# Rows of maxima from ScalarE's queue, seven projection steps a round, and gaps that end with a query group

## The chip, the cores and the metric

One core of one Trainium2 chip runs the kernel. The metric is the device time of one execution in microseconds; the runs shown are a median of three. Engines are called as in the profile: PE is TensorE (PEld its weight loads), DVE is VectorE, ACT is ScalarE, POOL is GpSimd, SP is SyncE, which issues most DMAs. A name with a q behind it (SPq, ACTq) is the engine's instruction queue.

## The reference

Four residual layers on one sequence of 2048 tokens with 576 features: sliding-window attention, a spectral filter, and both again with the same weights.

```python
def _A_ref(x, wqkv, wo):
    H = 32; Dh = D // H; W = 256                     # D = 576, Dh = 18
    qkv = (x @ wqkv).reshape(B, S, 3, H, Dh)          # -> q, k, v
    scores = einsum("bhqd,bhkd->bhqk", q, k) * (Dh ** -0.5)
    mask = (0 <= idx_q - idx_k) & (idx_q - idx_k < W)
    p = softmax(where(mask, scores, -1e9))
    return einsum("bhqk,bhkd->bhqd", p, v).reshape(B, S, D) @ wo

def _B_ref(x, w_r, w_i):
    X = rfft2(x) * (w_r + 1j * w_i)
    return irfft2(X, s=(S, D))

x = x + _A_ref(_layernorm(x), wqkv, wo)
x = x + _B_ref(_layernorm(x), w_r, w_i)
x = x + _A_ref(_layernorm(x), wqkv, wo)
x = x + _B_ref(_layernorm(x), w_r, w_i)
```

## The kernel before, in words

The attention layer (`layer_a`) is called twice; the spectral layer (`layer_b`) follows each. Only `layer_a` is touched.

**Tiles and head groups.** The 32 heads are worked in 8 groups `n` of four heads; a head of a group is named by `pair` and `hp`. The sequence has 16 tiles of 128 tokens. A tile of a group has a running number `x` = 16·n + i, 128 in all. Four tiles make a chunk `c` of 512 tokens.

**Projections.** A list `pj` holds the matmuls that make q and k: one *group* of 14 steps (128×512 each, line 798) for each block of 128 columns (i) and chunk (c). The groups of i = 0 and 1 are done first; the other 28 groups, 392 steps, are in `pj`. After its last step ScalarE casts the group to a high part `sg` (line 810), and a closure is put aside that subtracts on VectorE (line 813) and writes both parts to DRAM as `qk_d` (line 815, from ScalarE's queue for i < 2, otherwise from SP's). `remainders` calls the closures put aside. `stack_load` (line 830) brings q and k of one head group and chunk back from DRAM to `qs` and `ks`: twelve DMAs from SP.

**Scores, twice.** `score_max` (S, line 855) multiplies q by k for 128 queries and up to 384 keys, and VectorE takes each query's maximum (line 857). When four tiles of a chunk have their maxima, `m_rows` (line 865) transposes them on TensorE (`tpm`), ScalarE negates them into `mt` (line 870), and four DMAs of 2 KB (line 875) put them as one more row into `qs`, for each of the four heads. `exps` (E, line 892) then multiplies k by q with that row, which subtracts the maximum, and ScalarE takes the exponential (line 893); GpSimd cuts the two edges of the window (lines 895, 898). The maxima run ahead of the exponentials by `LEAD` = 10 tiles.

**Values.** `part` (line 912) adds one tile's products of P and V into the PSUM bank U. Four tiles of queries make a query group; at its end ScalarE copies U to `us` (line 917), and the next group writes U again. `norm` (line 926) transposes `us`, divides and stores.

**Order of the work.** The order is written out by hand. Every engine works its instructions in program order.
- `opening` (line 966): ten rounds, each with the four S of one tile and a share of the projection steps; before, 75 steps in ten rounds, eight and seven in turn. `m_rows` for chunks 0 and 1 of group 0 comes at the ends of rounds 4 and 8 (counted from 0).
- `bursts` (line 992): 158 bursts `k`, each of one S, three E, two S, and then a filling: value parts in some bursts, otherwise projection steps (14 to a gap of two to four bursts; in the first gap, bursts 0 to 3, nine steps), with at most two tasks (`m_rows` or `norm`) after the first two steps. `m_rows` for chunk 2 of group 0 is the task of burst 3, that for chunk 3 of burst 8. Bursts 4, 7, 9, ... hold value parts. When the projections are used up, from burst 137 on, parts are spread over all bursts, up to a length of 430 a burst (`took`).
- After them the last tiles (x ≥ 118), then the output projection (`Out`), which runs on into the spectral layer.

**Banks.** PSUM tags: `E` and `S` have three banks each, `pj` and `U` one. `turned` (line 860) chooses the bank of the transposes by how many steps are `done`: `E` before 75, then `S`, and `pj` when the projections are over. Group (i = 3, c = 0), the fifth of `pj`, stands in an `E` bank until its remainder has been taken.

Of the kernel before, what the change touches and what calls it, by code (L numbers as in the profile page):

```python
# [8 lines left out]
F32 = mybir.dt.float32  # L9
# [6 lines left out]
S, D = 2048, 576  # L16
DF = 289
NF = 290
NT = 16
# [589 lines left out]
def layer_a(tc, ident, eps, bp, src, dst, wqk_d, wv_d, wo_d, dc_d, gc_d, dram, copy, wvs, second, spectral, share):  # L609

    nc = tc.nc
# [15 lines left out]
    if True:  # L627
# [134 lines left out]
        with ExitStack() as c2:  # L762
# [9 lines left out]
            for j in range(2):  # L772
                q = wp.tile([128, 2, S], F32R, name=f"qs{j}", bufs=1)
                k = wp.tile([128, 2, S], F32R, name=f"ks{j}", bufs=1)
# [5 lines left out]
            def remainders():  # L780
                while ended:
                    ended.pop(0)()
# [60 lines left out]
            def score_max(x, pair, hp):  # L843

                n, i = divmod(x, NT)
                c, t = divmod(i, 4)
                q, k = qs[n % 2], ks_[n % 2]
                if (n, c) not in ms:
                    ms[n, c] = wp.tile([128, 2, 2, 4], F32, tag="m", name=f"m{n}_{c}", bufs=3)
                lo, hi = max(0, i - 2) * 128, (i + 1) * 128  # L850
                N = hi - lo
                b = 64 * hp
                four = x < LEAD and pair == hp == 1
                ps = pp.tile([128, 512], F32, tag="U" if four else "S", name=f"S{x}_{pair}_{hp}", bufs=1 if four else 3)
                T.matmul(ps[:, 0:N], q[b:b + 63, pair, i * 128:i * 128 + 128], k[b:b + 63, pair, lo:hi], start=True, stop=True)  # L855
                jk = wp.tile([128, 384], BF, tag="jk", name=f"jk{x}_{pair}_{hp}", bufs=3)
                V.tensor_tensor_reduce(out=jk[:, 0:N], in0=ps[:, 0:N], in1=mask[:, 384 - N:384], scale=1.0, scalar=-3e38,  # L857
                                       op0=ALU.add, op1=ALU.max, accum_out=ms[n, c][:, hp, pair, t:t + 1])

            def turned(name):  # L860

                tag = "E" if done < 75 else "S" if done < len(pj) else "pj"
                return pp.tile([128, 4, 128], F32, tag=tag, name=name, bufs=1 if tag == "pj" else 3)

            def m_rows(n, c):
                q = qs[n % 2]
                tp = turned(f"tpm{n}_{c}")
                T.transpose(tp[0:16, 0], ms[n, c].rearrange("p a b t -> p (a b t)"), ident)
                mt = wp.tile([16, 128], F32R, tag="mt", name=f"mt{n}_{c}", bufs=2)
                A.activation(mt, tp[0:16, 0], AF.Copy, scale=-1.0)  # L870
                for hp in range(2):
                    for pair in range(2):
                        r = (hp * 2 + pair) * 4
                        b = 64 * hp + 63
                        nc.sync.dma_start(q[b:b + 1, pair, c * 512:c * 512 + 512].rearrange("a (t q) -> a t q", t=4).bitcast(F32),
                                          mt[r:r + 4].bitcast(F32))

            pt = {}
# [70 lines left out]
            LEAD = 10  # L949
            pj = [f for i in range(2, 9) for c in range(4) for f in proj(i, c, c % 2 if i == 2 else c == 0 and i == 3)]  # L950
            done, due = 0, []
# [3 lines left out]
            def loads(t):  # L955
                if t + LEAD in (0, 2):
                    stack_load(0, 2 + (t + LEAD) // 2)
                n, c = divmod(t + 20, NT)
                if c % 4 == 0 and 0 < n < NQ:
                    stack_load(n, c // 4)  # L960
                if t + LEAD == 5:
                    v_load(0)
                if t + 12 in range(NT, NX, NT):
                    v_load((t + 12) // NT)

            def opening():

                n = 0
                for t in range(-LEAD, 0):
                    loads(t)  # L970
                    for pair in range(2):
                        for hp in range(2):
                            score_max(t + LEAD, pair, hp)
                    remainders()
                    want = -(-75 * (t + LEAD + 1) // LEAD)
                    yield from pj[n:want]
                    n = want
                    y = t + LEAD - 1
                    if y > 0 and y % 4 == 3:
                        m_rows(0, y // 4)  # L980

            def lasting(p):
                x, half = p
                i = x % NT
                return 0 if i == 0 else 216 if half else 432

            def source(p):
                x, half = p
                i = x % NT
                return x - 1 if half == 0 else x - 2 + 2 * (i % 2)  # L990

            def bursts():

                es = [(x, pair, hp) for x in range(MIX) for pair in range(2) for hp in range(2)]
                ss = [(x + LEAD, pair, 1 - hp) for x, pair, hp in es]
                parts = [(x, half) for x in range(MIX - 2) for half in range(2) if x % NT]
                values = {(4 * x + 7) // 3 + 2 for x in range(0, MIX - 2, 2)}
                ends = [3] + [max(k - 1 for k in values if k - 1 <= 4 + 134 * (i + 1) // 22) for i in range(22)]
                steps = {}
                for i, end in enumerate(ends):  # L1000
                    ks = [k for k in range(ends[i - 1] + 1 if i else 0, end + 1) if k not in values]
                    m = 14 if i else 9
                    steps.update({k: m // len(ks) + (z < m % len(ks)) for z, k in enumerate(ks)})
                at = 75
                for k in range(-(-len(es) // 3)):
                    e, c = es[3 * k:3 * k + 3], ss[3 * k:3 * k + 3]
                    for x, pair, hp in e:
                        if pair == hp == 0:
                            loads(x)
                            assert not any(source(p) == x - 6 for p in parts)  # L1010
                    score_max(*c[0])
                    for f in e:
                        exps(*f)
                    for f in c[:0:-1]:
                        score_max(*f)
                    remainders()

                    new, took = [], 0
                    spread = at == len(pj)
                    while parts and (took < 430 or source(parts[0]) < e[0][0] - 3 if spread else took == 0 or parts[0][0] % 2 or parts[0][1]):  # L1020
                        if (4 * source(parts[0] if spread else (parts[0][0] | 1, 1)) + 3) // 3 + 2 > k:
                            break
                        x, half = parts.pop(0)
                        part(x, half)
                        took += lasting((x, half))
                        if half and x % 4 == 3:
                            new.append((norm, *divmod(x // 4, 4)))

                    due.sort(key=lambda z: z[0] is norm)
                    tasks = [] if took and not spread else due[:1 + (len(due) > 2)]  # L1030
                    del due[:len(tasks)]
                    n = steps.get(k, 0)
                    for f in pj[at:at + min(2, n)]:
                        yield f
                    for f, *a in tasks:
                        f(*a)
                    for f in pj[at + 2:at + n]:
                        yield f
                    at += n

                    full = (3 * k + len(e)) // 4 + LEAD - 1
                    if (3 * k) // 4 + LEAD - 1 < full and full % 4 == 3:
                        new.append((m_rows, *divmod(full // 4, 4)))
                    due.extend(new)
                    for x, pair, hp in e:
                        if pair == hp == 1:
                            behind(x)
                remainders()
                assert at == len(pj)
                for p in parts:  # L1050
                    part(*p)
                    if p[1] and p[0] % 4 == 3:
                        due.append((norm, *divmod(p[0] // 4, 4)))
# [32 lines left out]
            for f in opening():  # L1086
                f()
                done += 1
            U = pp.tile([128, 512], F32, tag="U", name="U", bufs=1)
            V.memset(U, 0.0)  # L1090
            for f in bursts():
                f()
                done += 1
# [89 lines left out]
```

## Time and profile before

| | |
|---|---|
| median of 3 runs | 1512.99 us (1512.7 to 1518.36) |
| the profiled execution | 1514.61 us |
| its span, first to last instruction | 1512.9 us |
| mean granted clock of TensorE | 0.988 |
| busy: PE, PEld, DVE, ACT, POOL | 95%, 73%, 64%, 52%, 41% |
| first attention layer: opening and bursts | from about 107 to 458 us |
| second attention layer: opening and bursts | from about 858 to 1210 us |

A timeline row has the start in us, the length in us, engine, line, operation, the tile written and the tile read, their shapes, how many instructions were merged, and in brackets the idle time before it with what ended it. A row by stretches has, for each engine, the busy time in us and the number of instructions in brackets, then the granted clock (1.00 is full), the mean busy share of the 16 DMA engines and GB/s. A row of one line's instructions has the shortest, the median and the longest duration in ns. In the page's groups of instructions the count is followed by the busy time in us, the mean length in ns, and the idle time before them with what ended most of it.

### The profile page before, as it was taken

Reading aid. Unit: us, or ns where it says so; the run is one execution under the profiler, and the core shown is the slowest. Engines: PE = TensorE matmul, PEld = TensorE weight load, DVE = VectorE, ACT = ScalarE, POOL = GpSimd, SP = SyncE. Lnnn points to the kernel's source line nnn. Section 1 sums busy time; section 2 is a strip of 40 time slices with the busy share of each in tenths; the row PEclk is TensorE's granted clock in tenths of the full one; section 3 lists DMA queues with packets and bytes.
Section 4 is the critical chain, followed back from the end, with each engine's and each line's share of the span. In section 5 each row is a group of like instructions: output and inputs, shape, how many; then the busy total and the mean of one; then the engine's idle time right before and its main releaser. Section 6 shows DMA issues by size and latency. Waiting matters only on the chain.

```text
span 1512.9 us, 34671 instructions
## 1 busy us (share of the span) xinstructions
PE 1441.3 (95%) x12124; PEld 1097.8 (73%) x12124; DVE 968.4 (64%) x3152; ACT 789.3 (52%) x1900; POOL 623.0 (41%) x1026
## 2 busy tenths in 40 slices
PE   7998999999999899999999989999999998999998
PEld 7975666666656799759999756666666467997698
DVE  5327787878883555457852468878788735555476
ACT  5522676666676444224454246667666654442243
POOL 2172445445455323153421824444443543322434
PEclk9998999999999999999999989999999999999999
DMA  6756556655545365767663565555544454657654
GB/s 193 200 167 207 166 160 197 186 170 168 159 143 164 111 215 187 233 213 239 244 173 92 186 209 159 166 158 157 156 146 136 122 160 139 209 188 246 211 200 142
DMA packets 203131, 267.64 MB, mean 177 GB/s; under 512 B 103182, under 2 KB 108302, under 8 KB 201998
## 3 DMA queue, kind: packets, MB, share of 16 engines
q1 hardware_dynamic: 194638, 245.44, 52.6%
q10 hardware_dynamic: 7680, 15.59, 3.0%
q0 software_dynamic: 640, 4.39, 1.1%
q8 instruction: 97, 1.59, 0.5%
q14 instruction: 76, 0.62, 0.1%
HBM read 166.71 MB, written 102.00 MB: 178 GB/s over the span
## 4 chain that ended last, share of the span: by engine, by line
PE 70%; DVE 7%; DMA 6%; ACT 4%; POOL 4%; issue 2%; SPq 1%; POOLq 0%; DVEq 0%; ACTq 0%
PE pj L798 15%; PE S L855 12%; PE U L912 11%; PE ops L555 6%; PE E L892 5%; PE vps L738 4%; PE pf L202 3%; PE pz L215 3%; PE pi L361 2%; PE tpo L926 2%; PE po L382 2%; DMA ofree<-yd 1%; DMA qs<-mt 1%; PE pq L313 1%; PE p L294 1%
## 5 line engine op out<-in xcount | busy, mean ns | idle before, releaser
L857 DVE CUSTOM_DVE_ANT_0 jk<-S,mask 128x384 bf16<-128x384 f32 (+2 forms) x1024 | 491.2, 529 | 134.7 <-PE E L892 74.7
L893 ACT ACTIVATE P<-E 128x384 f32<-128x384 f32 (+2 forms) x1024 | 409.1, 475 | 180.5 <-PE E L892 151.9
L895 POOL TENSOR_SCALAR_AFFINE_SELECT P<-P 128x512 f32<-128x512 f32 x256 | 162.4, 634 | 386.9 <-ACT P L893 353.4
L855 PE MATMUL S<-ks,qs 63*128 63x384 f32 (+2 forms) x1024 | 281.4, 375 | 1.7 <-DVE m L857 0.5
L892 PE MATMUL E<-qs,ks 64*128 64x384 f32 (+2 forms) x1024 | 222.4, 374 | 12.1 <-DMA qs<-mt 10.0
L855 PEld LDWEIGHTS S<-ks,qs 63*128 63x128 f32 x1024 | 144.5, 187 | 114.2 <-DVE m L857 74.3
L912 PE MATMUL U<-P,vq 128*19 128x128 f32 (+1 forms) x3840 | 190.4, 331 | 4.4 <-ACT us L917 2.7
L798 PE MATMUL pj<-xh,wqh 128*128 128x512 f32 x360 | 156.8, 435 | 2.5 <-ACT vt L742 1.7
L912 PEld LDWEIGHTS U<-P,vq 128*19 128x19 f32 x3840 | 96.1, 99 | 82.4 <-issue 22.6
L898 POOL TENSOR_SCALAR_AFFINE_SELECT P<-P 128x512 f32<-128x512 f32 x224 | 142.0, 634 | 0.0
L892 PEld LDWEIGHTS E<-qs,ks 64*128 64x128 f32 x1024 | 110.9, 187 | 25.5 <-issue 13.8
L798 PE MATMUL pj<-xh,wql 128*128 128x512 f32 x360 | 128.1, 425 | 0.7 <-POOL wql L460 0.7
L555 PE MATMUL ops<-oroom 128*128 128x288 f32 x840 | 120.8, 299 | 4.4 <-DVE oroom L538 3.0
L798 PE MATMUL pj<-xl,wqh 128*128 128x512 f32 x288 | 120.1, 417 | 0.0
L555 PEld LDWEIGHTS ops<-oroom 128*128 128x128 f32 x840 | 112.8, 189 | 6.2 <-DVE oroom L538 3.9
L798 PEld LDWEIGHTS pj<-xh,wqh 128*128 128x128 f32 x360 | 67.9, 189 | 34.3 <-issue 11.4
L171 POOL TENSOR_TENSOR eo<-xn 128x287 f32<-128x287 f32 x32 | 26.1, 817 | 152.9 <-ACT xn L169 141.8
L813 DVE TENSOR_TENSOR sg<-pj,sg 128x512 fp32r<-128x512 f32 x72 | 49.5, 687 | 58.3 <-ACT sg L810 58.3
L857 DVE DVE_READ_ACCUMULATOR2_ANT m<- 128x1 f32 x1024 | 84.8, 83 | 0.0
L361 PE MATMUL pi<-oroom 128*128 128x256 f32 (+1 forms) x576 | 77.4, 289 | 5.9 <-ACT oroom L346 4.7
L798 PEld LDWEIGHTS pj<-xh,wql 128*128 128x128 f32 x360 | 64.2, 190 | 24.2 <-issue 12.8
L361 PEld LDWEIGHTS pi<-oroom 128*128 128x128 f32 (+1 forms) x576 | 73.1, 187 | 7.6 <-ACT oroom L346 5.6
(177 smaller groups left out, 2569.0 us busy)
## 6 DMA issues: line engine op xcount, KB each, us to landing
qk_d<-sg SPq DMA_DIRECT2D x56, 512.0 KB
qs<-qk_d SPq DMA_DIRECT2D x384, 72.0 KB
ks<-qk_d SPq DMA_DIRECT2D x384, 72.0 KB
v_d<-vt SPq DMA_DIRECT2D x32, 304.0 KB
vq<-v_d SPq DMA_DIRECT2D x16, 608.0 KB
yd<-ye SPq DMA_DIRECT2D x32, 290.0 KB
wt<-in_w SPq DMA_DIRECT2D x16, 580.0 KB
x<-ofree SPq DMA_DIRECT2D x32, 288.0 KB
```

The lines of the kernel that those rows point to most:

```text
L361: T.matmul(o, z[:, sl, c, lo:lo + m], mo, start=k == 0, stop=k == 5)
L555: self.nc.tensor.matmul(self.ps[u][n][:, 0:288], x, self.w[p][:, wk * D + n * 288:wk * D + n * 288 + 288], start=first and i == 0, stop=la ...
L738: T.matmul(ps[:, n, 0:288], xT(xk, c), w[:, wk, n * 288:(n + 1) * 288], start=i == 0, stop=i == len(ks) - 1)
L798: T.matmul(box["ps"].rearrange("r (n p) -> r n p", n=NT) if second else box["ps"], w[:, wk], x, start=s == 0, stop=s == len(ks) - 1)
L813: V.tensor_sub(rest[:, 1], by, rest[:, 0].bitcast(F32))
L855: T.matmul(ps[:, 0:N], q[b:b + 63, pair, i * 128:i * 128 + 128], k[b:b + 63, pair, lo:hi], start=True, stop=True)
L857: V.tensor_tensor_reduce(out=jk[:, 0:N], in0=ps[:, 0:N], in1=mask[:, 384 - N:384], scale=1.0, scalar=-3e38, op0=ALU.add, op1=ALU.max, accu ...
L892: T.matmul(ps[:, 0:nq], k[b:b + 64, pair, j * 128:j * 128 + 128], q[b:b + 64, pair, j * 128:j * 128 + nq], start=True, stop=True)
L893: A.activation(p[:, hl_, 0:nq], ps[:, 0:nq], AF.Exp, scale=SC)
L895: P.affine_select(out=p[:, :, 0:128], in_=p[:, :, 0:128], pattern=[[0, 4], [1, 128]], compare_op=ALU.is_ge, fill=0.0, base=0, channel_mult ...
L898: P.affine_select(out=p[:, :, 256:384], in_=p[:, :, 256:384], pattern=[[0, 4], [-1, 128]], compare_op=ALU.is_gt, fill=0.0, base=0, channel ...
L912: T.matmul(U[32 * h:32 * h + 19, (q0 % 4) * 128:(q0 % 4) * 128 + 128 * (q1 - q0)], vts[n][:, j, h], pt[n, j][:, h, (q0 - j) * 128:(q1 - j) ...
```

## The change

Three edits in `layer_a`.
- `m_rows`: the four DMAs of a row are issued by ScalarE when the head group is 0 and the chunk is 0, 1 or 2; by SP otherwise.
- `opening` and `bursts`: seven projection steps in each of the ten rounds (70 in all), and 14 in the first gap (four, four, three and three in bursts 0 to 3) as in the others. `turned` and the start of the bursts' counter go from 75 to 70 with it.
- `bursts`: a gap with value parts already in it ends before the first half of a tile that opens a query group (x % 4 == 0) or a head group's first computed tile (x % 16 == 1).

```diff
-                tag = "E" if done < 75 else "S" if done < len(pj) else "pj"
+                tag = "E" if done < 70 else "S" if done < len(pj) else "pj"
...
-                        nc.sync.dma_start(q[b:b + 1, pair, c * 512:c * 512 + 512].rearrange("a (t q) -> a t q", t=4).bitcast(F32),
+                        (nc.sync if n or c == 3 else nc.scalar).dma_start(q[b:b + 1, pair, c * 512:c * 512 + 512].rearrange("a (t q) -> a t q", t=4).bitcast(F32),
                                           mt[r:r + 4].bitcast(F32))
...
-                    want = -(-75 * (t + LEAD + 1) // LEAD)
+                    want = 7 * (t + LEAD + 1)
...
-                    m = 14 if i else 9
-                    steps.update({k: m // len(ks) + (z < m % len(ks)) for z, k in enumerate(ks)})
-                at = 75
+                    steps.update({k: 14 // len(ks) + (z < 14 % len(ks)) for z, k in enumerate(ks)})
+                at = 70
...
-                        x, half = parts.pop(0)
+                        x, half = parts[0]
+                        if took and half == 0 and (x % 4 == 0 or x % NT == 1):
+                            break
+                        parts.pop(0)
                         part(x, half)
```

## The prediction

> **What bounds the kernel now.** I read the page first: the chain of work that ended last, by engine, and the groups of instructions with what ended the idle time before them.
>
> ```profile
> PE 70%; DVE 7%; DMA 6%; ACT 4%; POOL 4%; issue 2%; SPq 1%; POOLq 0%; DVEq 0%; ACTq 0%
> L892 PE MATMUL E<-qs,ks 64*128 64x384 f32 (+2 forms) x1024 | 222.4, 374 | 12.1 <-DMA qs<-mt 10.0
> ```
>
> TensorE carries 70% of the chain, and the change neither adds nor removes a matmul. So only two things can move the time: holes in TensorE's row, and the clock at which it works. The second line names one hole that the change touches: 10.0 us in which E (the scores that go to the exponential) waited for the rows of maxima, which travel as `qs<-mt`. The timeline of TensorE shows where it lies, once in each attention layer:
>
> ```profile
> 137.59 0.62 PE L892 MATMUL E<-qs,ks 64*128 64x384 f32 x2
> 142.68 0.66 PE L892 MATMUL E<-qs,ks 64*128 64x384 f32 x1 [4.47 <-DMA qs<-mt]
> ...
> 891.78 0.65 PE L892 MATMUL E<-qs,ks 64*128 64x384 f32 x1 [5.07 <-DMA qs<-mt]
> ```
>
> That E is the ninth of its layer (burst 2, third of the burst): the first one that reads query tile 4, so the first that needs row group c=1. The timelines of ScalarE and of SyncE's queue show why the row is late:
>
> ```profile
> 130.87 0.27 ACT L870 ACTIVATE mt<-tpm 16x128 fp32r<-16x128 f32 x1 [3.01 <-PE tpm L868]
> ...
> 130.77 2.17 SPq L830 DMA_DIRECT2D qs<-qk_d  x6
> 132.99 3.23 SPq L830 DMA_DIRECT2D ks<-qk_d  x6
> 136.42 0.90 SPq L815 DMA_DIRECT2D qk_d<-sg  x2
> 137.41 3.30 SPq L875 DMA_DIRECT2D qs<-mt  x4
> ...
> 879.24 0.27 ACT L870 ACTIVATE mt<-tpm 16x128 fp32r<-16x128 f32 x1 [3.10 <-PE tpm L868]
> 887.47 3.29 SPq L875 DMA_DIRECT2D qs<-mt  x4
> ```
>
> The row is ready in SBUF at 131.14 (130.87 + 0.27). Its four DMAs stand in SP's queue behind twelve loads of the next head group and two writes of projections, and are issued from 137.41 to 140.71. TensorE goes on at 142.68, 1.97 us after the last issue. In the second layer 7.96 us pass between 879.51 and 887.47. So the wait is made on the queue, not by the transfer.
>
> The stretches by granted clock show a second loss behind the first:
>
> ```profile
> 141.00:142.00 1.00, 0.00 (x0) 0.00 (x0) 0.00 (x0) 0.00 (x0) 0.00 (x0) 0.60 0.26 94
> 150.00:151.00 1.00, 1.00 (x10) 0.82 (x6) 0.57 (x2) 0.16 (x1) 0.00 (x0) 0.50 0.01 3
> ...
> 888.00:889.00 1.00, 0.00 (x0) 0.00 (x0) 0.00 (x0) 0.00 (x0) 0.77 (x2) 0.85 1.04 358
> 898.00:899.00 1.00, 1.00 (x16) 0.35 (x8) 1.00 (x5) 0.51 (x2) 0.00 (x0) 0.53 0.52 199
> ```
>
> The columns are TensorE, weight loads, VectorE, ScalarE, GpSimd, then the clock, the DMA share and GB/s. During the wait the clock falls to 0.50, and it stays there to past 151 and near 899, long after work has resumed: 8.3 us of work at half speed in the first layer (142.68 to 151) and 7.2 us in the second.
>
> **The change part by part.** (1) *Queue.* For head group 0 the rows c=0, 1, 2 leave from ScalarE. With c=1 no longer behind SP's loads, the issue can begin at about 131.1. SP in turn gets to its loads about 3 us earlier each time it passes such a row; nothing on an engine waits for those loads in this stretch. c=0 was in time before and can only come earlier; c=3 stays on SP, where it was in time. The price of one issue:
>
> ```profile
> L815 SPq DMA_DIRECT2D qk_d<-sg x56: 365/389/2587, 125.4 to 1178.5; - x56
> L815 ACTq DMA_DIRECT2D qk_d<-sg x16: 361/366/404, 88.4 to 857.8; - x16
> L875 SPq DMA_DIRECT2D qs<-mt x256: 572/573/2399, 127.3 to 1217.2; - x128
> ```
>
> No row shows `qs<-mt` on ScalarE. The like transfer costs the same on both engines (389 against 366 ns), so I take SP's median, 573 ns, plus about 45 ns between two: four take 2.5 us. The ends are 1.5 us (four of 366 ns) and 9.6 us (four of SP's longest, 2399 ns). With 2.5 us of issue and the 1.97 us to landing, c=1 lands near 135.6, before burst 2 wants it at about 138. The two stalls go: −4.47 and −5.07 us.
>
> The Trainium skill, "DMA: Bandwidth & Descriptors", section "Issuing engines are not separate DMA queues", speaks against this: all issuers share the same 16 DMA engines, and a second issuer saves only sequencer time, usually small. Here sequencer time is the larger part, 6.27 us from 131.14 to 137.41 against 1.97 us to landing; by the page's "usually" the gain would be little, and no row of before shows this DMA on the other queue.
>
> (2) *Clock.* If the hole goes, so does the slow stretch. Burst starts (the single S at the head of each) price it:
>
> ```profile
> 144.74 0.69 PE L855 MATMUL S<-ks,qs 63*128 63x384 f32 x1
> 147.36 0.69 PE L855 MATMUL S<-ks,qs 63*128 63x384 f32 x1
> ...
> 150.08 0.69 PE L855 MATMUL S<-ks,qs 63*128 63x384 f32 x1
> 152.74 0.44 PE L855 MATMUL S<-ks,qs 63*128 63x384 f32 x1
> 154.82 0.44 PE L855 MATMUL S<-ks,qs 63*128 63x384 f32 x1
> ```
>
> Bursts 5 and 6 both hold five projection steps: 2.66 us, most of it slow, against 2.08 at full clock. Burst 3 took 2.62 us and burst 4 2.72; at full clock I estimate 1.7 (two steps and the row's transpose: 2.08 less three steps of 0.26, rounded up for the transpose and for what VectorE needs) and 1.85 (16 U, some 1.1 us by the rows of U in (5), in place of five steps). The rest of burst 2 (142.68 to 144.74) took 2.06, about 1.1 at full clock. Together 0.58 + 0.92 + 0.87 + 0.96 = 3.3; I take −3.0 in the first layer, and −2.7 in the second, where burst 5 is fast already. The ends are 0 and half of the slow work, −4.2 and −3.6.
>
> The Trainium skill, "TensorE: Matmul & The Clock Gate", section "What's actually happening", has the clock return after one busy window of about 3.4 us. By it the slow work would be worth at most half of 3.4 us, 1.7 a layer. The trace disagrees: 8.3 us.
>
> (3) *The new load on ScalarE.* Its queue is in order, so what stands behind an issue waits. c=0 and c=1 fall into the opening, where ScalarE idles (3.01 us ahead of the row above). Behind c=1 stand one cast of a projection and the first exponential; the issues end about 0.4 us after the cast could start. c=2 falls into burst 3:
>
> ```profile
> 147.25 0.58 ACT L810 CAST sg<-pj 128x512 fp32r<-128x512 f32 x1 [0.50 <-PE pj L798]
> 147.74 0.26 ACT L870 ACTIVATE mt<-tpm 16x128 fp32r<-16x128 f32 x1
> ...
> 150.84 1.26 ACT L893 ACTIVATE P<-E 128x384 f32<-128x384 f32 x3 [1.46 <-PE E L892]
> 153.25 1.26 ACT L893 ACTIVATE P<-E 128x384 f32<-128x384 f32 x3 [1.16 <-PE E L892]
> ```
>
> Burst 3 now has three steps with the row's transpose after the second, so the cast too comes behind the four issues: the three exponentials of burst 4 start 2.5 + 0.6 = 3.1 us later than the row's own end. E has three banks, so burst 5's first E waits for burst 4's first exponential. ScalarE's slack is 1.16 to 1.46 us a burst. I take 3.1 less about 1.1: +2.0 us a layer. The ends: 0 if the queue takes the issues beside other work, and +8.5 (9.6 less 1.1).
>
> (4) *Seven steps a round.* The opening loses five steps. Three heads of its rounds, the first wait of burst 0, and the page's groups of VectorE:
>
> ```profile
> 123.10 0.62 PE L855 MATMUL S<-ks,qs 63*128 63x384 f32 x4
> 125.72 0.62 PE L855 MATMUL S<-ks,qs 63*128 63x384 f32 x4
> 128.08 0.62 PE L855 MATMUL S<-ks,qs 63*128 63x384 f32 x4
> 134.17 0.44 PE L892 MATMUL E<-qs,ks 64*128 64x384 f32 x1 [0.43 <-ACT P L893]
> ...
> L857 DVE CUSTOM_DVE_ANT_0 jk<-S,mask 128x384 bf16<-128x384 f32 (+2 forms) x1024 | 491.2, 529 | 134.7 <-PE E L892 74.7
> L813 DVE TENSOR_TENSOR sg<-pj,sg 128x512 fp32r<-128x512 f32 x72 | 49.5, 687 | 58.3 <-ACT sg L810 58.3
> ```
>
> Eight steps make 2.62 us, seven 2.36: 0.26 a step, −1.3 in all. VectorE needs four maxima of 0.48 us (491.2 over 1024) and, every second round, 0.69 for a remainder: 2.27 on average, so it stays just under 2.36. The same five steps come back in bursts 0 to 3, +1.3 less what holes there swallow: 0.43 us in burst 0, where E waits for an exponential to free its bank, and perhaps as much in burst 1. ScalarE's 0.4 us from (3) eats part of it. I count (4) as 0; ends −0.9 (two such holes filled) and +0.4. From burst 4 on the steps lie where they lay.
>
> (5) *Gaps that end with a query group.* By the loop's own conditions the order changes only in bursts 141 to 150 of each layer, after the projections. There two bursts of a layer start the next group's part right behind the last part of the one before, and wait for U to be copied (both of the first layer, and the first of the second):
>
> ```profile
> 431.71 0.63 PE L912 MATMUL U<-P,vq 128*19 128x256 f32 x8 [0.85 <-ACT us L917]
> 440.05 0.63 PE L912 MATMUL U<-P,vq 128*19 128x256 f32 x8 [0.85 <-POOL P L898]
> ...
> 1182.20 1.05 PE L912 MATMUL U<-P,vq 128*19 128x256 f32 x8 [0.85 <-ACT us L917]
> ```
>
> At most −1.7 us a layer. Against it: two parts move into burst 150, which had none, and there ScalarE is full:
>
> ```profile
> 451.00:452.00 1.00, 1.00 (x11) 0.39 (x11) 0.86 (x5) 1.00 (x4) 1.00 (x2) 1.00 0.00 0
> ```
>
> I take −1.0 a layer; ends −1.7 and +0.6 (one part of 0.63 that nothing hides).
>
> **Sum.** First layer: −4.47 − 3.0 + 2.0 + 0 − 1.0 = −6.5. Second: −5.07 − 2.7 + 2.0 + 0 − 1.0 = −6.8. Together −13.3 us. The profiled execution took 1514.61 us with a span of 1512.9; I expect a span near 1499.6. The median of the runs shown, 1512.99, is 1.6 below the profiled execution; taken from it, the forecast is **1499.7**.
>
> **Rivals.**
> - *Issues cost ScalarE nothing that TensorE sees.* Then the +2.0 goes in both layers: 1495.7. For it: idle time of over 1 us a burst. Against: the cast stands behind the issues too. 14%.
> - *The new wait slows the clock.* A hole of 2 us in burst 5 could be enough, as holes of that sum were in the second layer:
>
> ```profile
> 1179.00:1182.00 3.00, 1.84 (x14) 0.91 (x14) 2.16 (x10) 2.29 (x6) 1.22 (x2) 1.00 0.79 228
> 1183.00:1185.00 2.00, 2.00 (x22) 1.31 (x22) 1.02 (x3) 1.06 (x3) 0.06 (x1) 0.50 0.44 156
> ```
>
> TensorE was busy 1.84 of 3 us and then ran at 0.50. About 1.5 to 2 us a layer: 1503.2. 17%. By the skill's clock page, same section, a whole idle window is needed and this rival would not occur; these two rows speak against that.
> - *The change does not do what it says:* the rows land late on the other queue as well, because the DMA engines are full of the loads that SP now issues earlier (share 1.04 at 888). If the stall is still 2 us with its slow clock, 9.5 − 4 and half of the clock term remain, and −5.5 − 2.9 + 4.0 − 2.0 = −6.4: 1506.6. 9%.
> - *Slower:* each of the four issues takes SP's longest, 2.4 us, on ScalarE. Then c=1 holds it 9.6 us and the first exponential is 7 us late, c=2 another 8.5, with slow clock behind both (3 each). A layer gains 8.6 ((1), (2) and (5)) and loses 7 + 8.5 + 6 = 21.5: +26 in all, 1539. It decides from a hold of about 6 us on, where the two delays, each less what fits beside them (2.5 and 1.1), make up the gain: 1.5 us an issue. Against it: ACTq's longest issue is 404 ns. 4%.
>
> The forecast keeps 56%. The range takes in the two neighbours and the part of the third that keeps half of the gain: **1494 to 1507**. A change under 0.5%, 7.6 us, can't be told from none here; so faster means below 1505.4: 56 + 14 + 17 and a third of 9, 0.88; the same 0.08; slower 0.04.
>
> **What would show it.** Right: no `qs<-mt` in front of E in bursts 2, clock 1.00 through both starts, bursts 3 to 6 near 2 us; `qs<-mt` rows of 0.57 us on ScalarE's queue; in burst 5 an E waiting about 2 us for an exponential; no 0.85 us hole ahead of U in bursts 141 and 145. Wrong: an idle time over 3 us around the first bursts, half clock there, or issue rows well over 0.6 us.

## The result and the profile after

The changed kernel is **slower**: 1524.98 us (median of 7 runs, 1520.35 to 1525.63) against 1516.19 us for the kernel before (7 runs, 1512.7 to 1519.42), a ratio of 1.0054 (95% interval 1.0035 to 1.0073). The profiled executions have spans of 1523.2 and 1512.9 us, so 10.3 us are to be found. The forecast was 13.3 us the other way.

The page's group of E, and the same line in the answer on waits (engine, line, what was waited for: us in total, times, longest), both of the changed kernel:

```profile
L892 PE MATMUL E<-qs,ks 64*128 64x384 f32 (+2 forms) x1024 | 222.3, 373 | 24.3 <-ACT P L893 22.8
```

```profile
PE E L892 <- DMA qs<-mt: 1.2, 2, 0.9
```

The stall that the change aimed at is gone: 10.0 us of waiting for `qs<-mt` have become 1.2. But E now waits 22.8 us for ScalarE. The timeline of TensorE, first of the kernel before and then of the changed one, shows where. The U rows are the value parts of bursts 4 and 7, the first two bursts that have any; they are the same work in both kernels and serve as milestones:

```profile
148.66 1.49 PE L912 MATMUL U<-P,vq 128*19 128x256 f32 x16
155.56 1.50 PE L912 MATMUL U<-P,vq 128*19 128x256 f32 x32
```

```profile
143.03 0.85 PE L912 MATMUL U<-P,vq 128*19 128x256 f32 x16
151.67 1.45 PE L892 MATMUL E<-qs,ks 64*128 64x384 f32 x3 [7.42 <-ACT P L893]
161.00 0.44 PE L892 MATMUL E<-qs,ks 64*128 64x384 f32 x1 [2.21 <-ACT P L893]
161.55 1.50 PE L912 MATMUL U<-P,vq 128*19 128x256 f32 x32
...
906.37 1.45 PE L892 MATMUL E<-qs,ks 64*128 64x384 f32 x3 [8.57 <-ACT P L893]
```

Burst 4 is reached at 143.03 in place of 148.66: **5.6 us ahead**. The forecast gain was there. Three bursts later it is lost twice over: burst 7 starts at 161.55 in place of 155.56, 6.0 us behind. By milestones, the changed kernel less the kernel before (in brackets the starts in the kernel before and in the changed one, layer by layer):

| milestone | layer 1 | layer 2 |
|---|---|---|
| U of burst 4 (148.66 and 143.03; 897.80 and 896.58) | −5.6 | −1.2 |
| U of burst 7 (155.56 and 161.55; 904.06 and 915.87) | +6.0 | +11.8 |
| first `tpz`, the spectral layer (484.37 and 487.90; 1236.43 and 1245.31) | +3.5 | +8.9 |
| end of the span | | +10.3 |

Between bursts 4 and 7 the first layer loses 11.6 us and the second 13.0; from there to the end of each layer, where the gaps that end with a query group lie, 2.5 and 2.9 us are won back.

What holds the exponentials? ScalarE and its queue in the changed kernel:

```profile
142.53 2.46 ACTq L875 DMA_DIRECT2D qs<-mt  x4
145.04 0.59 ACT L810 CAST sg<-pj 128x512 fp32r<-128x512 f32 x1 [2.58 <-PE S L855]
151.12 2.52 ACT L893 ACTIVATE P<-E 128x384 f32<-128x384 f32 x6 [5.50 <-DMA qk_d<-sg]
...
160.46 0.49 ACT L893 ACTIVATE P<-E 128x384 f32<-128x384 f32 x1 [3.02 <-DMA qk_d<-sg]
```

The four issues of row c=2 take 2.46 us, as forecast. The 5.50 us after the cast are something else: the exponentials of burst 4 wait until a *write of a projection* to DRAM has landed. The code says why. The tile `P` of the exponentials and the first projection results `sg` (4·i + c < 13) share one tag of six buffers, so an exponential that begins a new `P` needs a buffer whose `qk_d<-sg` is complete. Those writes are issued by SP, here in the changed kernel:

```profile
115.03 5.17 SPq L830 DMA_DIRECT2D qs<-qk_d  x6
120.25 5.06 SPq L830 DMA_DIRECT2D ks<-qk_d  x6
...
129.52 4.95 SPq L830 DMA_DIRECT2D ks<-qk_d  x6
134.56 1.07 SPq L815 DMA_DIRECT2D qk_d<-sg  x2
...
137.71 6.82 SPq L830 DMA_DIRECT2D qs<-qk_d  x6
...
147.28 0.90 SPq L815 DMA_DIRECT2D qk_d<-sg  x2
```

The first pair of writes leaves at 134.56 and the second at 147.28. The kernel before:

```profile
114.58 2.17 SPq L830 DMA_DIRECT2D qs<-qk_d  x6
116.79 2.75 SPq L830 DMA_DIRECT2D ks<-qk_d  x6
...
125.36 0.89 SPq L815 DMA_DIRECT2D qk_d<-sg  x2
```

There the first pair left at 125.36 and the second at 136.42 (shown in the prediction). SP, relieved of twelve DMAs a layer, is 9 and 11 us **later**: from 115 to 147 us four of its six groups of six loads take 4.95 to 6.82 us, where the kernel before needs 2.2 to 3.2 for each. Its waits between 110 and 150 us, in the changed kernel:

```profile
SPq L830 <- DMA qs<-mt: 5.9, 4, 2.5
SPq L830 <- DMA qs<-qk_d: 5.8, 4, 2.5
```

SP's loads wait for `qs<-mt`, the rows that were taken off its queue, although they read nothing of them. The program's list of SP's instructions, with the semaphore for which each waits, shows the link (the number in front only counts the rows, the number behind DMAHW is the semaphore's; changed kernel, two columns):

```
64 L639 DMACopy wqr<-in_wqk   [waits DMAHW1]    71 L830 DMACopy ks<-qk_d [waits DMAHW4]
65 L830 DMACopy qs<-qk_d      [waits DMAHW2]    72 L830 DMACopy ks<-qk_d [waits DMAHW5]
66 L830 DMACopy qs<-qk_d      [waits DMAHW3]    73 L830 DMACopy ks<-qk_d [waits DMAHW6]
67 L830 DMACopy qs<-qk_d      [waits DMAHW4]    74 L830 DMACopy ks<-qk_d [waits DMAHW7]
68 L830 DMACopy qs<-qk_d      [waits DMAHW5]    75 L830 DMACopy ks<-qk_d [waits DMAHW0]
69 L830 DMACopy qs<-qk_d      [waits DMAHW0]    76 L830 DMACopy ks<-qk_d [waits DMAHW1]
70 L830 DMACopy qs<-qk_d      [waits DMAHW3]
```

In this program the DMAs of SP and ScalarE take eight completion semaphores in turn, in program order, and each waits until the DMA that had the same one before is complete. In SP's own sequence 6, 7, 1 and 2 are left out between rows 68 and 70: the row c=0, on ScalarE's queue, has them. So rows 73, 74, 76 and 77 of SP can't be issued before a row of maxima that ScalarE issues at 121.06, and which TensorE, VectorE and ScalarE have to make first; and between two such points SP has four semaphores left in place of eight. A DMA on ScalarE's queue was taken from SP's queue, but not from its order. The Trainium skill, "DMA: Bandwidth & Descriptors", section "Why a DMA increments its semaphore by 16 and not by 1", says why a program needs such waits: two DMAs in flight must not share a semaphore, since the count can then be full before the first has landed. No run here shows such a mix-up; what the runs show is the price of the wait.

The stretches of the changed kernel (same columns as in the prediction) show the two prices:

```profile
132.00:134.00 2.00, 1.39 (x7) 0.67 (x5) 1.82 (x7) 0.59 (x2) 0.00 (x0) 1.00 0.05 17
...
146.00:148.00 2.00, 0.00 (x0) 0.00 (x0) 0.82 (x3) 0.00 (x0) 0.00 (x0) 0.55 0.41 137
148.00:150.00 2.00, 0.00 (x0) 0.00 (x0) 0.00 (x0) 0.00 (x0) 0.00 (x0) 0.50 0.92 341
...
154.00:156.00 2.00, 2.00 (x7) 1.16 (x7) 0.23 (x2) 0.00 (x0) 0.17 (x1) 0.50 0.59 190
```

From 132 to 134 the DMA engines are nearly idle (0.05) while SP's queue stands; the hole of 7.42 us drops the clock to 0.50, and it stays there to 156, as it did behind the old stall.

### The profile page after: what moved, and what is told of

Same layout as the page of the kernel before. It is cut to its first block, busy times and chain, and to the rows that moved or that the text cites. A ratio compares the mean times of both kernels' runs of the same rounds, so it can differ in the third digit from the quotient of the medians.

```text
span 1523.2 us, 34662 instructions
## 1 busy us (share of the span) xinstructions
PE 1443.2 (95%) x12124; PEld 1102.5 (72%) x12124; DVE 968.4 (64%) x3152; ACT 789.7 (52%) x1900; POOL 622.9 (41%) x1026
## 4 chain that ended last, share of the span: by engine, by line
PE 68%; DVE 8%; DMA 6%; POOL 5%; ACT 4%; issue 2%; SPq 2%; ACTq 0%; POOLq 0%; DVEq 0%
PE pj L798 15%; PE S L855 12%; PE U L912 10%; PE ops L555 6%; PE E L892 5%; PE vps L738 4%; PE pf L202 3%; PE pz L215 3%; PE pi L361 2%; PE tpo L926 2%; PE po L382 2%; DVE ofree L298 1%; POOL uv L302 1%; POOL uv L303 1%; DMA qs<-mt 1%
## 5 line engine op out<-in xcount | busy, mean ns | idle before, releaser
L892 PE MATMUL E<-qs,ks 64*128 64x384 f32 (+2 forms) x1024 | 222.3, 373 | 24.3 <-ACT P L893 22.8
L555 PE MATMUL ops<-oroom 128*128 128x288 f32 x840 | 123.9, 304 | 4.4 <-DVE oroom L538 3.0
L555 PEld LDWEIGHTS ops<-oroom 128*128 128x128 f32 x840 | 115.9, 193 | 6.2 <-DVE oroom L538 4.0
L810 ACT CAST sg<-pj 128x512 fp32r<-128x512 f32 x72 | 42.4, 588 | 67.7 <-PE pj L798 52.3
```

What stands on the lines that cost most here:

```text
L555: self.nc.tensor.matmul(self.ps[u][n][:, 0:288], x, self.w[p][:, wk * D + n * 288:wk * D + n * 288 + 288], start=first and i == 0, stop=la ...
L892: T.matmul(ps[:, 0:nq], k[b:b + 64, pair, j * 128:j * 128 + 128], q[b:b + 64, pair, j * 128:j * 128 + nq], start=True, stop=True)
```

## The experiments

**Theory A** is the chain just read: rows on ScalarE hold back SP's loads through the shared turn of semaphores; SP's writes, behind those loads, come late; `P` finds no buffer; E stands; the clock halves. **Rival B**: the 2.5 us of issues on ScalarE are themselves the loss, and SP's lateness is harmless. **Rival C**: the seven steps or the ends of the gaps do the harm. **Rival D**, in the second round: SP's late loads hold the work directly, the buffers are a side effect; some of the expectations give the letter D to another rival, which they name. "Before" is below always the kernel before on the same chip.

### The queue alone

The kernel before with only the first edit (`nc.sync if n or c == 3 else nc.scalar`).

> The kernel before with the first edit alone: rows c=0, 1, 2 of head group 0 from ScalarE's queue. Theory A (completion slots): each transfer of the SP and ScalarE queues waits for the transfer eight places before it in the program's common rotation to be complete; the rows on ScalarE stand in SP's rotation among loads that SP reaches earlier, so SP falls behind by 7 to 9 us, writes the projections late, and the exponentials, whose P buffers are the same ones that hold the projections (sg), wait 6 to 9 us for those writes in bursts 4 to 7. Then this kernel is slower than before by 9 to 14 us, as the changed kernel is once the gain of the gaps is taken out, and SP's first write of a projection (line 815) starts about 9 us later than the 125.4 us of before. Rival B (a busy ScalarE): the wait is the 2.5 us of issues themselves, SP is not late, and the time is between 5 us faster and 3 us slower than before. Rival C (the steps): the harm comes from the seven-step rounds, so without them this is faster by 5 us or more.

The time measured is 1530.91 us (before 1515.35), ratio 1.0113 (1.0084 to 1.0143). ScalarE, and SP's second pair of writes:

```profile
152.56 2.66 ACT L893 ACTIVATE P<-E 128x384 f32<-128x384 f32 x6 [8.01 <-DMA qk_d<-sg]
```

```profile
149.19 0.90 SPq L815 DMA_DIRECT2D qk_d<-sg  x2
```

The first edit alone makes the loss, by the same wait: 15.6 us against before, somewhat more than the 9 to 14 expected and more than the 8.8 us of the whole change.

### The other two edits alone

The changed kernel with `nc.sync` in `m_rows` again.

> The changed kernel with the first edit undone: all rows from SP, seven steps a round, gaps that end with a query group. Theory A: the old stall behind the rows of c=1 is back (4 to 5 us a layer, half clock behind it), SP runs as before, no exponential waits for a write; the gaps gain about 2 us a layer: 1 to 6 us faster than before. Rival B says the same. Rival C (the steps do the harm): slower than before by 5 us or more.

The time measured is 1512.51 us (before 1515.35), ratio 0.9987 (0.9967 to 1.0007). The old stall stands as it stood:

```profile
141.48 0.66 PE L892 MATMUL E<-qs,ks 64*128 64x384 f32 x1 [4.08 <-DMA qs<-mt]
```

The 2.8 us won are inside the expected range, and the interval takes in no change. Rival C, which asked for a loss of 5 us or more, falls.

### The rows from GpSimd

```diff
-(nc.sync if n or c == 3 else nc.scalar).dma_start(q[b:b + 1, ...
+(nc.sync if n or c == 3 else nc.gpsimd).dma_start(q[b:b + 1, ...
```

GpSimd's DMAs take semaphores of their own, and in this program SP's sequence runs through all eight without a gap.

> The changed kernel, but the twelve rows' DMAs a layer are issued by GpSimd instead of ScalarE. GpSimd's transfers have completion slots of their own, so SP's rotation is untouched. Theory A: SP is on time or early, rows are in time, neither the stall of before nor that of the changed kernel is there: 12 to 18 us faster than before, first write of a projection by SP at about 125 us or earlier. Rival B: the same, since ScalarE has no issues. Rival D (the transfer itself is late on any queue but SP's, because the 16 DMA engines are full): E still waits 2 us or more for the rows in burst 2 and the time is within 5 us of before.

The time measured is 1510.54 us (before 1515.35), ratio 0.9963 (0.9943 to 0.9982). SP's first two pairs of writes leave 2 and 3 us after those of before, in place of 9 and 11. No E waits for a row, so rows from another queue need not be late, as the rival D of this expectation had it:

```profile
127.72 0.89 SPq L815 DMA_DIRECT2D qk_d<-sg  x2
...
139.33 0.90 SPq L815 DMA_DIRECT2D qk_d<-sg  x2
```

But only 5 us are won, less than the 12 to 18 expected, and the timeline of ScalarE names the rest:

```profile
151.26 0.49 ACT L893 ACTIVATE P<-E 128x384 f32<-128x384 f32 x1 [3.94 <-DMA qk_d<-sg]
```

The third pair of writes, which leaves at 147.40 behind 24 loads of the next head group, now comes too late for `P`. In the kernel before this wait lay hidden behind the stall for the row: when TensorE comes 6 us earlier, the next thing that is late shows. Removing the old stall needs SP's writes earlier as well.

### Only the row c=1 from ScalarE

```diff
-(nc.sync if n or c == 3 else nc.scalar)
+(nc.scalar if n == 0 and c == 1 else nc.sync)
```

> The changed kernel, but only the row c=1 goes from ScalarE's queue; c=0 and c=2 go from SP. Theory A: only four slots are ever held by ScalarE, once, so SP falls behind by about half as much, 3 to 5 us less whatever it loses to issuing the other rows; the wait of an exponential for a write shrinks to 0 to 4 us; the time lies between the changed kernel and before or a little under before: -6 to +4 us. Rival B: ScalarE issues nothing inside the bursts, so neither stall is there: 10 us or more faster than before.

The time measured is 1524.11 us (before 1515.35), ratio 1.0066 (1.0038 to 1.0093). The mechanism on SP is A's; the size was not, and the wait that it leads to is another. Four DMAs are enough; SP and TensorE:

```profile
124.82 9.73 SPq L830 DMA_DIRECT2D ks<-qk_d  x6
...
135.81 2.76 SPq L875 DMA_DIRECT2D qs<-mt  x4
```

```profile
139.32 1.10 PE L892 MATMUL E<-qs,ks 64*128 64x384 f32 x2 [6.82 <-DMA qs<-mt]
```

One group of six loads takes 9.73 us, since it holds a load that waits for the row of c=1, and the row of c=0, now behind it on SP, becomes the late one. ScalarE issues no row in the bursts here, and E waits for a row from SP, so B can't explain the loss.

### The writes from GpSimd, the rows still from ScalarE

```diff
-(nc.scalar if i < 2 else nc.sync).dma_start(qk_d[...
+(nc.scalar if i < 2 else nc.gpsimd if 4 * i + c < 13 else nc.sync).dma_start(qk_d[...
```

This cuts the chain at its second link.

> The changed kernel with one more edit: the first five writes of projections (i=2, and i=3 with c=0), whose tiles share buffers with P, leave from GpSimd's queue in place of SP's; the rows stay on ScalarE. Theory A (SP falls behind because its DMAs wait for the rows', and the writes behind SP's loads hold P's buffers): SP's loads are as late as in the changed kernel (groups of six at about 5 us), but the exponentials no longer wait for qk_d<-sg; the 7.4 us hole before E goes, and with it the half clock; 12 to 20 us below the changed kernel, 1505 to 1513. Rival D (SP's late loads themselves hold the work, the buffers are a side effect): another wait of 4 us or more in its place, within 5 us of the changed kernel, 1520 to 1530.

The time measured is 1518.4 us (before 1515.67), ratio 1.0016 (1.0 to 1.0031): 7 us below the changed kernel in place of 12 to 20, and above the range that A expected. No exponential waits for `qk_d<-sg` any more, so that link is right. SP is as slow as in the changed kernel, and two other things are late. The waits left in front of TensorE in the first layer, and the stretches of the second of them:

```profile
130.35 0.59 PE L855 MATMUL S<-ks,qs 63*128 63x384 f32 x3 [2.22 <-DMA qs<-qk_d]
...
148.93 1.45 PE L892 MATMUL E<-qs,ks 64*128 64x384 f32 x3 [1.86 <-ACT P L893]
```

```profile
146.00:148.00 2.00, 1.07 (x17) 0.42 (x9) 1.12 (x6) 0.10 (x1) 0.37 (x1) 1.00 0.37 127
148.00:150.00 2.00, 1.07 (x4) 0.78 (x5) 1.17 (x3) 2.00 (x5) 0.00 (x0) 0.78 0.18 53
150.00:152.00 2.00, 2.00 (x6) 1.35 (x5) 1.04 (x4) 0.90 (x3) 1.22 (x2) 0.50 0.53 164
...
154.00:156.00 2.00, 2.00 (x8) 1.41 (x5) 1.39 (x6) 1.68 (x4) 1.24 (x3) 0.51 0.51 170
```

S waits 2.22 us for a late load: D holds for a part. And the 1.86 us are rival B's price, without the buffers in front of it: the exponentials behind the four issues of c=2, as the prediction had them. The clock behind that short hole is 0.50 to 156. From U of burst 4 to U of burst 7 this kernel needs 11.30 us (145.85 to 157.15). The second layer has the same hole, 1.87 us at 895.42 with 0.50 from 897 to 900, and needs 10.08 us (892.33 to 902.41).

### Rows and writes from GpSimd

Both edits together.

> As the run before, but the rows leave from GpSimd too. Theory A: neither wait is left (no row late, no buffer held, SP not slowed): the hole of 3.2 us before E that stood with the rows alone on GpSimd goes, with half clock behind it; 3 to 8 us below that run's 1510.5, so 1502 to 1508, about what the prediction gave to the change. Rival D: no lower than 1509, since GpSimd's nine issues of about 0.5 us more hold its cuts of P.

The time measured is 1499.3 us (before 1515.67), ratio 0.989 (0.9857 to 0.9923), 3 us below the expected range. No hole over 0.6 us is left before E in either start. GpSimd's issues cost nothing that shows.

### The rows from GpSimd, the loads four tiles later

```diff
-                n, c = divmod(t + 20, NT)
+                n, c = divmod(t + 16, NT)
```

This edit goes on the kernel with the rows from GpSimd: a load of a later head group is issued 16 tiles before its use, and the first writes pass ahead of it.

> The changed kernel with the rows on GpSimd's queue, and every load of a later head group four tiles later (16 tiles ahead of its use in the loop in place of 20). Theory A: SP issues the first writes of projections before those loads, about 6 us earlier, so no exponential waits for a buffer; 1502 to 1508. Rival D: the later loads are missed by the maxima of the next head group (S waits for qs or ks at the start of group 1), 1510 or more.

The time measured is 1495.07 us (before 1515.67), ratio 0.987 (0.9841 to 0.9899), 7 us below the expected range; run again, it took 1496.2 us (below). SP's second pair of writes leaves at 130.32, and from 140 to 154 TensorE works at full clock. U of bursts 4 and 7:

```profile
142.65 0.85 PE L912 MATMUL U<-P,vq 128*19 128x256 f32 x16
148.76 1.50 PE L912 MATMUL U<-P,vq 128*19 128x256 f32 x32
```

It takes 6.11 us from one to the other, where the changed kernel needs 18.52.

### The rows on SP, the loads four tiles later

The changed kernel with `nc.sync` in `m_rows`, and the edit of `loads` above.

> The changed kernel with the rows back on SP's queue and every load of a later head group four tiles later. Theory A: the row c=1 finds SP's queue empty at about 131, as on ScalarE, but no load waits for it: neither the old stall (4.5 and 5.1 us) nor the new one, 1502 to 1508. Rival D: the row c=2 or the loads of group 1 become late in its place, 1510 or more.

The time measured is 1501.2 us (before 1515.67), ratio 0.9901 (0.9873 to 0.9928), 1 us below the expected range. No second queue is needed for most of the gain: what made the row late was the loads ahead of it, and they can wait. One small wait is left in layer 1:

```profile
139.62 0.41 PE L892 MATMUL E<-qs,ks 64*128 64x384 f32 x1 [1.04 <-DMA qs<-mt]
```

### The rows on ScalarE, the loads four tiles later

> The changed kernel (rows on ScalarE) with every load of a later head group four tiles later. Theory A: SP still waits for the rows, but its writes now come ahead of the loads, so no P buffer is held and no E waits for 7 us; what is left is the price of the issues on ScalarE, a hole of about 2 us in front of an E in burst 5 of each layer with half clock behind it (2 to 3 us more): 1499 to 1508, so 4 to 10 above the same kernel with the rows on GpSimd. Rival D: the loads of SP are still the bound, 1512 or more.

The time measured is 1511.87 us (before 1514.73), ratio 0.9989 (0.9969 to 1.0008): above the range that A expected and at the edge of its rival's. The expected price of the issues is there, a hole of 1.82 us in each layer with half clock behind it (0.50 from 148 to 150 in the first layer, whose hole this is):

```profile
145.53 1.20 PE L892 MATMUL E<-qs,ks 64*128 64x384 f32 x3 [1.82 <-ACT P L893]
```

The rest is A's wait again. Two pairs of writes now come ahead of the loads, the third does not. ScalarE, and then SP:

```profile
153.75 0.49 ACT L893 ACTIVATE P<-E 128x384 f32<-128x384 f32 x1 [3.17 <-DMA qk_d<-sg]
```

```profile
138.24 8.82 SPq L830 DMA_DIRECT2D qs<-qk_d  x6
...
149.35 0.90 SPq L815 DMA_DIRECT2D qk_d<-sg  x2
```

The six loads at 138.24 take 8.82 us: they wait for the row c=2, issued at 142.00. With the rows from GpSimd, and nothing else changed, it is 1496.2 on the same chip: 16 us for the choice of the queue.

### What the other two edits are worth, without the stalls

Three kernels on one chip, all with the rows from GpSimd and the later loads: one with the third edit undone, one with the second undone, and one with both kept.

> Rows on GpSimd and later loads, with the third edit undone (value gaps may run over the end of a query group). Where no hole of the start stands beside it, the edit's own worth shows: the two holes of 0.85 us before U come back in the first layer, one in the second. By the prediction 2.0 us above the kernel with the edit; by the traces so far (2.4 in the first layer) 3 to 5 above it.

> Rows on GpSimd and later loads, with the second and the third edit undone (75 steps in the opening). By the prediction the steps are worth nothing: the same as the kernel with only the third edit undone, within 2 us. If seven steps a round are worth something by themselves, 3 us or more above it.

> Rows on GpSimd, later loads, both other edits as in the changed kernel: the base for the two runs before, on the same chip. 1494 to 1498 by the earlier run of it (1495.07).

The second kernel differs from its expectation's words: it undid only the steps (75 in the opening) and kept the third edit, so it is to be compared with the last one. The times measured (before 1514.73) are, without the ends, 1499.44 (ratio 0.9901, 0.9875 to 0.9927), with 75 steps 1497.79 (0.9896, 0.9867 to 0.9924), with both edits 1496.2 (0.9878, 0.9848 to 0.9907). Undoing the ends costs 3.2 us between the medians and undoing the steps 1.6, as far as expected, but the intervals overlap. The traces say more on the ends. TensorE without them, and then with them, between the same two transposes:

```profile
415.89 0.66 PE L926 MATMUL tpo<-ident,us 128*128 128x128 f32 x4 [0.62 <-DVE sg L813]
423.77 0.63 PE L912 MATMUL U<-P,vq 128*19 128x256 f32 x8 [0.85 <-ACT us L917]
432.11 0.63 PE L912 MATMUL U<-P,vq 128*19 128x256 f32 x8 [0.85 <-POOL P L898]
...
452.17 0.66 PE L926 MATMUL tpo<-ident,us 128*128 128x128 f32 x4 [0.70 <-ACT us L917]
```

```profile
416.84 0.66 PE L926 MATMUL tpo<-ident,us 128*128 128x128 f32 x4 [0.62 <-DVE sg L813]
...
450.70 0.66 PE L926 MATMUL tpo<-ident,us 128*128 128x128 f32 x4 [0.69 <-ACT us L917]
```

These are 36.28 against 33.86 us: the ends of the gaps are worth 2.4 us in this layer, more than the two holes of 0.85, and 1.8 us in the second (1159.07 to 1195.54 without them, 1157.22 to 1191.88 with them). For the steps, 1.6 us between two medians is too little for these runs to tell from nothing.

## Why the prediction was wrong

**The step that failed** is in (1): "SP in turn gets to its loads about 3 us earlier each time it passes such a row; nothing on an engine waits for those loads in this stretch". The first half is wrong: SP got 9 to 11 us later, by the semaphores that its DMAs share with ScalarE's. The second half holds for the loads of the changed kernel and leaves out what stands behind them: no matmul waited for a load there (S did in one experiment, 2.22 us), but the *writes behind the loads* on SP's queue came late, and with them the buffers that `P` shares with `sg`. SP's delay, which the sum has at nothing, is the main part of the 11.6 and 13.0 us lost between bursts 4 and 7: E waited 7.42 and 8.57 us there for exponentials, most of it for want of a buffer (5.50 us of ScalarE's time in layer 1), and half clock followed. The prediction counted what the rows waited for on the queue; it did not ask what else stands on that queue, which tile each of those DMAs releases, and who wants that tile next. The trace of before shows no wait of ScalarE for `qk_d<-sg` in this stretch, so the link could only be found in the tags of the code.

The other steps:
- **(1), rest**: right. The stall for c=1 went, the issues on ScalarE took 588 ns (median) in place of the estimated 573, a row of four 2.46 to 3.14 us, and layer 1 stood 5.6 us ahead at burst 4.
- **(2)**: right in kind. Half clock behind the old stall went, and came back behind the new one. Kernels without either show the whole size: burst 7 starts 6.8 us earlier than before (148.76 against 155.56). Of it 4.5 are the stall; the other 2.3 stand where the forecast had 3.0 for the clock.
- **(3)**, +2.0 a layer: the hole was there, 1.82 to 1.87 us in both layers of the two kernels where no buffer hid it (the writes from GpSimd, and the later loads), but the half clock behind it had been given to a rival. From burst 4 to 7, with the writes from GpSimd, 11.30 us against 6.11 make 5.2 us in layer 1, and 10.08 against 6.22 (880.08 to 886.30) make 3.9 in layer 2. The rival "the new wait slows the clock" was right about this; less the hole, 3.3 and 2.0 us are left, where it had 1.5 to 2 a layer.
- **(4)**, 0: not refuted; 1.6 us between two medians is all that shows.
- **(5)**, −1.0 a layer: right in kind and too small; 2.4 and 1.8 us by the pairs above, outside its ends.
- **The rivals**: the slower one had the wrong cause: it needed 1.5 us an issue, and the issues took 0.588. "Late because the DMA engines are full" was wrong as well; where SP stood their share *fell* (0.05 of their time from 132 to 134, 0.74 in the kernel before). No rival had a second queue that slows the first. The Trainium skill's sentence in "DMA: Bandwidth & Descriptors", section "Issuing engines are not separate DMA queues", that a second issuer saves only sequencer time, pointed to a small gain; here the second issuer cost the first one its pace, 9 and 11 us.
- **The chances**: 56, 14, 17 and a third of 9 make 0.90 for a faster kernel, not 0.88. Nothing else hangs on that sum.

That the semaphores' turn is the link, and not some other thing that the two queues share, rests on the program's list of waits, on SP's waits for `qs<-mt`, and on the rows from GpSimd, which have the same bytes and other semaphores. No run changed the order of the turn itself, and GpSimd differs from ScalarE in its queue as well.

## What to carry to other kernels

Before a DMA is moved to another engine's queue, read which completion semaphores the program gives it, and what the old queue will then wait for: a DMA that waits for data not yet made can hold up a queue that it no longer stands in. When a stall of several us is removed, ask what the traffic behind it releases (buffers by their tag, not only by their name), since the next wait stands hidden behind the first. Here the cheaper edit was to move what stands ahead of the late transfer: loads issued four tiles later, with the rows left where they were, gave 1501.2 us, and with the rows on GpSimd 1495.07 to 1496.2, a ratio to the kernel before of 0.987 (0.9841 to 0.9899) and 0.9878 (0.9848 to 0.9907).

## What the runs showed of the hardware

- Half clock can follow a hole of 1.8 to 1.9 us: TensorE was busy 1.07 of 2 us twice around the hole of 1.86, and then ran at 0.50 to 156; holes of 1.82 and 1.87 did the same. The length alone does not decide: behind the hole of 2.21 us before 161.00 in the changed kernel, and behind one of 1.97 in its second layer, the clock stayed at 1.00.

```profile
160.00:161.00 1.00, 0.00 (x1) 0.00 (x1) 0.00 (x0) 0.55 (x2) 0.00 (x0) 1.00 0.53 154
161.00:162.00 1.00, 1.00 (x12) 0.55 (x16) 0.49 (x3) 1.00 (x3) 0.36 (x1) 1.00 0.47 176
```

- The Trainium skill, "TensorE: Matmul & The Clock Gate", section "What's actually happening", asks for an idle window of about 3.4 us before half clock; the holes of 1.82 to 1.87 us speak against it.
- One DMA of a row of maxima (four segments of 512 bytes) took its issuer a median of 588 ns on ScalarE, 573 on SP (the kernel before) and 518 on GpSimd. The first row is of the changed kernel, the second of the one with the rows on GpSimd and the later loads.

```profile
L875 ACTq DMA_DIRECT2D qs<-mt x24: 580/588/1199, 121.1 to 898.0; - x24
```

```profile
L875 POOL DMA_DIRECT2D qs<-mt x24: 518/518/694, 121.1 to 882.1; - x24
```
